# Issuing block 0's mask work earlier: one copy moved up on ScalarE, one product moved ahead of two weight loads on GpSimd

## The chip, the cores and the metric

The kernel runs on one core of one Trainium2 chip. The metric is the device time of one execution in microseconds (us). "The span" is the time from the first to the last recorded instruction of the profiled execution; it is some 2 us shorter than the device time. Every run also has a mean granted TensorE clock, where 1.0 is full speed.

The engines are called as the profile calls them: PE (TensorE matmul), PEld (its weight loads), DVE (VectorE), ACT (ScalarE), POOL (GpSimd), SP (SyncE).

## The reference

A linear attention with decay (4 batches, 8 heads, 768 positions, head size 64) is followed by a gated feed-forward layer on 3072 tokens (512 to 1536 to 512). Cut to what matters:

```python
intra = einsum(q_blk, k_blk) * Dmask        # decayed causal scores inside a block
intra = einsum(intra, v_blk)
inter = einsum(q_blk * lam_pow, kv_state)   # state from earlier blocks; zero for block 0
out   = intra + inter
...
gate = 1 / (1 + exp(-(x @ w_gate)));  val = x @ w_val
return (gate * val) @ w_out
```

## The kernel before

The kernel works in six blocks of 128 positions. The program gives each engine a list of instructions, and POOL's records up to 32 us start in the order of its list. In block 0 the attention has to be finished for all four batches before the first dense matmul (`gp`, the gate product; `vp` is the value product) can start. The stretch up to there is called the ramp below, and `ft` counts the slices of 128 of the 1536 columns; one load of WG or WV, called a weight slice, holds two of them. A load has landed when its data are in place. One batch goes through these steps:

- `piece_tq0`, `piece_tk0`: PE transposes q and k; DVE and ACT copy them out of PSUM as QS and KS.
- `piece_s`: PE computes the scores `sp`, in two halves (two heads that share a partition block).
- `piece_m` or `piece_m2`: the scores times the mask give `MT`. `piece_m` does both halves on DVE. `piece_m2` does half 0 on DVE; half 1 is copied from PSUM by ACT (`sc`) and multiplied by POOL.
- `piece_a`: PE multiplies by v (`op`), ACT copies the result into `XT`, which the dense matmuls read.

POOL also issues the loads of q, k, v and of the weights. That takes it 0.7 to 1.2 us each for most of them, and its products queue between these issues (the trace below has 0.76 to 0.81 us for a weight issue).

```python
    def piece_m2(n, b):
        MT[n, b] = mtp.tile([128, 2, HP, C], BF16, tag="MT", name="MT")
        nc.vector.tensor_tensor(out=MT[n, b][:, 0], in0=SP[n, b][0], in1=mask[:, 0], op=ALU.mult)
        sc = const.tile([128, HP, C], FP32, tag="sc", bufs=2)
        nc.scalar.copy(sc, SP[n, b][1])
        nc.gpsimd.tensor_tensor(out=MT[n, b][:, 1], in0=sc, in1=mask[:, 1], op=ALU.mult)
    # ...
    GW = DFF // 6
    load_gv(0, GW)            # weights WG, WV of ft 0 and 1: two DMA issues on POOL
    # ... transposes and scores of batch 0 (cut)
    piece_s(0, [1])
    piece_tk0(1)              # k of batches 2 and 3: two KS copies on ACT
    piece_tq0([2])
    piece_m2(0, 1)
    load_gv(1, GW)
    load_gv(2, GW)
    idle(3)                   # dummy matmuls on zeros
    piece_tq0([3])
    piece_s(0, [2], ps_ff, "ff")
    piece_m2(0, 2)
    piece_s(0, [3])
    piece_m(0, 3)
    idle(3)
    piece_a(0, [0])
    piece_a(0, [1])
    idle(2)
    piece_a(0, [2])
    piece_a0(3)
    idle(2)
    make_kd(0)                # POOL
    # ... further loads (cut), then the dense part
    gv(0, 0, 1, 2, 3)         # per ft: four gp matmuls, sigmoid, four vp matmuls, product
```

Of the kernel before, what the change touches and what calls it, by code (L numbers as in the profile page):

```python
# [11 lines left out]
ALU = mybir.AluOpType  # L12
# [4 lines left out]
def kernel(  # L17
# [11 lines left out]
    nc = tc.nc  # L29
# [52 lines left out]
    def load_gv(i, w):  # L82
        fs = slice(i * w, (i + 1) * w)
        nc.gpsimd.dma_start(out=WG[:, :, fs], in_=wg_r[:, :, fs])  # L84
        nc.gpsimd.dma_start(out=WV[:, :, fs], in_=wv_r[:, :, fs])  # L85
# [43 lines left out]
    for hp in range(HP):  # L129
# [6 lines left out]
    mask = const.tile([128, 2, HP, C], FP32, tag="mask")  # L136
    nc.vector.tensor_tensor(out=mask, in0=tri.unsqueeze(1).unsqueeze(1).to_broadcast([128, 2, HP, C]),
                            in1=pk.rearrange("p (g u) -> p u g", u=2).unsqueeze(3).to_broadcast([128, 2, HP, C]),
                            op=ALU.mult)
# [3 lines left out]
    def idle(n):  # L143
        for i in range(n):
            nc.tensor.matmul(wm, lhsT=zero[:, :128], rhs=zero, start=True, stop=True,  # L145
                             skip_group_check=True)

    QS, KS, MT, XT, KD = {}, {}, {}, {}, {}
# [12 lines left out]
    def piece_tq0(bs):  # L161
        tq = ps_at.tile([128, 2, HP, C], BF16, name="tq", tag="ps")
        for b in bs:
            if (0, b // 2) not in QS:
                QS[0, b // 2] = trsb.tile([128, 2, HP, C], BF16, tag="QS", name="QS")
            for hp in range(HP):
                nc.tensor.transpose(tq[:, b % 2, hp, :], Q[0][:, b, 2 * hp:2 * hp + 2, :], ident)
        for b in bs:
            nc.vector.tensor_tensor(out=QS[0, b // 2][:, b % 2], in0=tq[:, b % 2], in1=lamq, op=ALU.mult)

    def piece_tk0(bp):
        tk = ps_at.tile([128, 2, HP, C], BF16, name="tk", tag="ps")
        for i in range(2):
            for hp in range(HP):
                nc.tensor.transpose(tk[:, i, hp, :], K[0][:, 2 * bp + i, 2 * hp:2 * hp + 2, :], ident)
        KS[0, bp] = trsb.tile([128, 2, HP, C], BF16, tag="KS", name="KS")
        for i in range(2):
            nc.scalar.copy(KS[0, bp][:, i], tk[:, i])  # L178
# [21 lines left out]
    SP, OP = {}, {}  # L200

    def piece_s(n, bs, pool=ps_at, tag="ps"):

        for b in bs:
            bp, i = b // 2, b % 2
            sp = [pool.tile([128, HP, C], FP32, name=f"sp{u}", tag=tag) for u in range(2)]
            for hp in range(HP):
                for u in range(2):
                    us = slice(u * 64, (u + 1) * 64)
                    nc.tensor.matmul(sp[u][:, hp, :], lhsT=KS[n, bp][us, i, hp, :],  # L210
                                     rhs=QS[n, bp][us, i, hp, :],
                                     start=(hp == 0), stop=(hp == HP - 1), skip_group_check=True)
            SP[n, b] = sp

    def piece_m2(n, b):
        MT[n, b] = mtp.tile([128, 2, HP, C], BF16, tag="MT", name="MT")
        nc.vector.tensor_tensor(out=MT[n, b][:, 0], in0=SP[n, b][0], in1=mask[:, 0], op=ALU.mult)
        sc = const.tile([128, HP, C], FP32, tag="sc", bufs=2)
        nc.scalar.copy(sc, SP[n, b][1])
        nc.gpsimd.tensor_tensor(out=MT[n, b][:, 1], in0=sc, in1=mask[:, 1], op=ALU.mult)  # L220

    def piece_m(n, b):
        MT[n, b] = mtp.tile([128, 2, HP, C], BF16, tag="MT", name="MT")
        for u in range(2):
            nc.vector.tensor_tensor(out=MT[n, b][:, u], in0=SP[n, b][u], in1=mask[:, u], op=ALU.mult)  # L225
# [110 lines left out]
    GW = DFF // 6  # L336
# [7 lines left out]
    piece_s(0, [0])  # L344
    piece_m(0, 0)
    piece_s(0, [1])
    piece_tk0(1)
    piece_tq0([2])
    piece_m2(0, 1)
    load_gv(1, GW)  # L350
    load_gv(2, GW)
    idle(3)
    piece_tq0([3])
    piece_s(0, [2], ps_ff, "ff")
    piece_m2(0, 2)
    piece_s(0, [3])
    piece_m(0, 3)
    idle(3)
# [154 lines left out]
```

## Time and profile before

| | before |
|---|---|
| device time, median of 3 runs at the time of the prediction | 238.61 us (237.46 to 238.71) |
| span of the profiled run | 236.2 us |
| PE busy | 226.0 us, 96% |
| longest stop of PE after its start | 2.63 us, 15.86 to 18.50 |
| time at half clock inside the kernel | 3.41 us, 18.83 to 22.25 |

The first view is the timeline of the kernel before. Columns: start us, length us, engine, line, operation, output<-input, shapes, count; in brackets the engine's idle time before it and what ended that.

```profile
12.21 0.60 ACT L219 COPY sc<-sp 128x512 f32<-128x512 f32 x1
12.90 1.27 POOL L220 TENSOR_TENSOR MT<-sc,mask 128x512 bf16<-128x512 f32 x1 [0.95 <-ACT sc L219]
13.31 0.59 ACT L219 COPY sc<-sp 128x512 f32<-128x512 f32 x1 [0.50 <-PE sp L210]
14.11 0.81 POOL L84 DMA_DIRECT2D WG<-in_moe_w_gate_dram  x1
14.92 0.76 POOL L85 DMA_DIRECT2D WV<-in_moe_w_val_dram  x1
15.65 0.77 POOL L84 DMA_DIRECT2D WG<-in_moe_w_gate_dram  x1
16.38 0.78 POOL L85 DMA_DIRECT2D WV<-in_moe_w_val_dram  x1
17.14 1.31 POOL L220 TENSOR_TENSOR MT<-sc,mask 128x512 bf16<-128x512 f32 x1
18.50 0.38 PE L238 MATMUL op<-MT,vb 128*64 128x128 bf16 x7 [2.63 <-POOL MT L220]
20.00 1.91 PE L297 MATMUL gp<-XT,WG 128*128 128x512 bf16 x4
21.71 1.29 PE L303 MATMUL vp<-XT,WV 128*128 128x512 bf16 x4
22.84 1.03 PE L297 MATMUL gp<-XT,WG 128*128 128x512 bf16 x4
```

Two things are to be seen. The input of POOL's second product, the second `sc`, is ready at 13.90, but the product starts at 17.14, because four weight issues stand ahead of it in POOL's program: for 3.2 us its data are ready, and it overtakes none of the issues. And the first `gp` and `vp` groups are slow: four `gp` take 1.91 us by their records, where the next four take 1.03.

The second view is the table by stretches. The columns are the stretch, its length, busy us (and count) of PE, PEld, DVE, ACT and POOL, the granted clock, the DMA share (the packets' times over the time of 16 engines; a share above 1, such as the 2.14 of the first line, means that packets overlap), and GB/s.

```profile
11.93:15.34 3.41, 3.22 (x45) 1.62 (x42) 3.19 (x6) 1.84 (x4) 2.46 (x4) 1.00 2.14 168
15.34:18.75 3.41, 0.78 (x12) 0.36 (x12) 0.00 (x0) 0.71 (x2) 3.41 (x5) 1.00 1.45 196
18.75:22.17 3.42, 3.42 (x21) 1.29 (x16) 0.42 (x1) 1.08 (x3) 3.42 (x2) 0.51 1.42 192
```

The clock records of the trace start at 5.18, 18.83 and 22.25 us: 1.0 for 13.653 us, 0.5 for 3.413, then 1.0 for 215.040. These lengths are 4, 1 and 63 times 3.413, so the instants lie on one grid of 3.413 us; its steps are called grid windows below. (The stretches shown were cut 0.08 us early, hence the 0.51.) In the grid window from 15.42 PE worked only 0.78 us; in the next window the clock is half. The three windows before, from 5.18, 8.59 and 12.01, held 2.10, 2.60 and 3.22 us of PE work, and none was followed by a drop. So PE's stop seems to cost twice: 2.63 us of waiting, and then slow matmuls (1.91 us against 1.03 for four `gp`).

### The profile page before, as it was taken

To read this page: it belongs to the slowest core of one execution; us is meant where nothing else is said; L and a number is where in the kernel's file an instruction comes from. 1 tells how busy PE (TensorE), PEld (TensorE's weight loads), DVE (VectorE), ACT (ScalarE), POOL (GpSimd) and SP (SyncE) were. 2 spreads that over 40 slices of the span, in tenths; PEclk is the share of its full clock that TensorE was granted. 3 is DMA by queue.
4 is the path that set the end of the run, shared out by engine and by line. 5 is a ranking of instruction groups with operands and counts; after the bars stand their busy time and mean duration, and the time that the engine had idled before them with its cause. 6 is when DMAs were issued, how large, how long until landed. Compare 5 with 4: busy or idle time off the path is not lost.

```text
span 236.2 us, 3854 instructions
## 1 busy us (share of the span) xinstructions
PE 226.0 (96%) x1554; PEld 115.8 (49%) x1554; DVE 106.0 (45%) x185; ACT 80.8 (34%) x147; POOL 84.3 (36%) x73
## 2 busy tenths in 40 slices
PE   7768999999999999999999999999999999999993
PEld 2433445688644455544455544455544455444441
DVE  4351485574674250654750654750654750243300
ACT  5542334545331133433223333223333224433220
POOL 8989997770199000398000398000000000000000
PEclk9997999999999999999999999999999999999999
DMA  9999999999935993939982749992730012100022
GB/s 58 143 180 157 159 190 158 199 180 157 142 68 70 170 215 125 158 67 88 157 69 89 164 62 85 156 72 89 160 66 0 0 44 92 44 0 3 0 89 89
DMA packets 102321, 24.89 MB, mean 105 GB/s; under 512 B 91552, under 2 KB 99232, under 8 KB 102304
## 3 DMA queue, kind: packets, MB, share of 16 engines
q0 software_dynamic: 82064, 14.16, 80.8%
q1 hardware_dynamic: 20240, 10.49, 19.8%
q8 instruction: 12, 0.20, 0.4%
q14 instruction: 5, 0.04, 0.1%
HBM read 28.32 MB, written 6.29 MB: 147 GB/s over the span
## 4 chain that ended last, share of the span: by engine, by line
PE 91%; POOL 3%; DMA 3%; ACT 1%; issue 1%; POOLq 0%
PE po L329 27%; PE gp L297 24%; PE vp L303 24%; PE vp L320 3%; PE op L238 3%; DMA kb<-in_k_dram 3%; PE gp L314 2%; PE sp L210 2%; PE op L231 2%; PE cp L277 2%; POOL MT L220 1%; POOL WG L84 1%; POOL WV L85 1%; POOL kb L78 0%; ACT KS L178 0%
## 5 line engine op out<-in xcount | busy, mean ns | idle before, releaser
L306 DVE TENSOR_TENSOR ht<-sg,vp 128x512 bf16<-128x512 bf16 x65 | 44.7, 688 | 87.0 <-PE vp L303 86.7
L297 PE MATMUL gp<-XT,WG 128*128 128x512 bf16 x260 | 67.7, 383 | 0.0
L303 PE MATMUL vp<-XT,WV 128*128 128x512 bf16 x260 | 67.0, 380 | 0.0
L329 PE MATMUL po<-WO,ht 128*128 128x512 bf16 x288 | 65.2, 379 | 0.0
L300 ACT ACTIVATE sg<-gp 128x512 bf16<-128x512 f32 x65 | 38.8, 597 | 75.9 <-PE gp L297 75.8
L329 PEld LDWEIGHTS <-ht 128*128 128x128 bf16 x288 | 27.1, 98 | 32.2
L303 PEld LDWEIGHTS <-WV 128*128 128x128 bf16 x260 | 25.6, 99 | 31.1 <-issue 0.8
L297 PEld LDWEIGHTS <-WG 128*128 128x128 bf16 x260 | 24.8, 99 | 27.8 <-issue 1.1
L269 POOL TENSOR_TENSOR sd<-Sb,dec 128x512 f32<-128x512 bf16 x16 | 16.2, 1038 | 56.9 <-DVE Sb L286 56.9
L225 DVE TENSOR_TENSOR MT<-sp,mask 128x512 bf16<-128x512 f32 x44 | 27.8, 683 | 13.7 <-PE sp L210 13.7
L332 ACT COPY ob<-po 128x512 f32<-128x512 f32 x24 | 14.1, 586 | 54.5 <-PE po L329 50.7
L260 POOL TENSOR_TENSOR kd<-kb,kds 128x2048 bf16<-128x2048 bf16 x5 | 18.1, 3626 | 2.8 <-DMA kb<-in_k_dram 2.8
L245 ACT CAST XT<-op 128x512 bf16<-128x512 f32 x23 | 12.4, 588 | 7.4 <-PE op L238 7.4
L286 DVE TENSOR_TENSOR Sb<-cp,sd 64x256 bf16<-64x256 f32 x32 | 13.4, 420 | 0.8
L78 POOL DMA_DIRECT2D qb<-in_q_dram x9 | 12.5, 1387 | 0.8 <-POOLq L497 0.8
L78 POOL DMA_DIRECT2D vb<-in_v_dram x9 | 12.2, 1368 | 0.0
L78 POOL DMA_DIRECT2D kb<-in_k_dram x8 | 11.5, 1442 | 0.0
L145 PE MATMUL wm<-zero 128*128 128x512 bf16 x26 | 9.2, 489 | 1.2 <-DVE zero L97 1.2
L238 PE MATMUL op<-MT,vb 128*64 128x128 bf16 x184 | 7.6, 222 | 2.6 <-POOL MT L220 2.6
L324 DVE TENSOR_TENSOR ht<-sg,vp 128x256 bf16<-128x256 bf16 x14 | 5.8, 420 | 6.2 <-PE vp L320 3.8
L320 PE MATMUL vp<-XT,WV 128*128 128x256 bf16 x56 | 8.4, 272 | 0.1
L314 PE MATMUL gp<-XT,WG 128*128 128x256 bf16 x56 | 8.4, 273 | 0.0
(58 smaller groups left out, 114.4 us busy)
## 6 DMA issues: line engine op xcount, KB each, us to landing
out_dram<-ob SPq DMA_DIRECT2D x24, 256.0 KB, 2.0
qb<-in_q_dram POOLq DMA_DIRECT2D x4, 512.0 KB, 7.9
kb<-in_k_dram POOLq DMA_DIRECT2D x4, 512.0 KB, 10.0
vb<-in_v_dram POOLq DMA_DIRECT2D x4, 512.0 KB, 12.5
WG<-in_moe_w_gate_dram POOLq DMA_DIRECT2D x6, 256.0 KB, 6.6
WV<-in_moe_w_val_dram POOLq DMA_DIRECT2D x6, 256.0 KB, 7.2
WO<-in_moe_w_out_dram POOLq DMA_DIRECT2D x3, 512.0 KB, 14.8
kb<-in_k_dram POOLq DMA_DIRECT2D x4, 256.0 KB, 6.2
```

Of the source, the lines that this page charges most:

```text
L78: nc.gpsimd.dma_start(out=t[:, b0:b1], in_=src[b0:b1, :, sl, :].rearrange("b h s d -> s (b h) d"))
L225: nc.vector.tensor_tensor(out=MT[n, b][:, u], in0=SP[n, b][u], in1=mask[:, u], op=ALU.mult)
L238: nc.tensor.matmul(OP[n, b][us, hp, :], lhsT=V[n][:, b, 2 * hp + u, :], rhs=MT[n, b][:, u, hp, :], start=(n == 0 and hp == 0), stop=(hp == ...
L260: nc.gpsimd.tensor_tensor(out=KD[n], in0=K[n], in1=kds.unsqueeze(1).unsqueeze(3).to_broadcast([128, B, H, D]), op=ALU.mult)
L269: nc.gpsimd.tensor_tensor(out=SD[b], in0=Sb[:, b], in1=dec.unsqueeze(2).to_broadcast([128, HP, 128]), op=ALU.mult)
L297: nc.tensor.matmul(gp, lhsT=WG[:, mt, fs], rhs=x[:, mt, :], start=(mt == 0), stop=(mt == NMT - 1))
L300: nc.scalar.activation(sg, gp, AF.Sigmoid)
L303: nc.tensor.matmul(vp, lhsT=WV[:, mt, fs], rhs=x[:, mt, :], start=(mt == 0), stop=(mt == NMT - 1))
L306: nc.vector.tensor_mul(HT[n, ft], sg, vp)
L320: nc.tensor.matmul(vp[:, cs], lhsT=WV[:, mt, fs], rhs=x[:, mt, cs], start=(mt == 0), stop=(mt == NMT - 1))
L329: nc.tensor.matmul(po, lhsT=HT[n, ft][:, tt * 128:(tt + 1) * 128], rhs=WO[:, ft, :], start=(ft == 0), stop=(ft == NFT - 1))
L332: nc.scalar.copy(ob, po)
```

## The change

The intent: POOL's two mask products should not wait behind things they do not need. ACT copies `sc` of batch 1 before the second pair of KS copies, so that POOL can start its first product earlier. POOL does its second product ahead of the last pair of weight issues, and no longer behind it. Nothing is added or removed. A listing of each engine's instructions shows that PE and DVE keep their order.

```diff
-    def piece_m2(n, b):
+    def piece_m2(n, b, part):
+        if part:
+            nc.vector.tensor_tensor(out=MT[n, b][:, 0], in0=SP[n, b][0], in1=mask[:, 0], op=ALU.mult)
+            return
         MT[n, b] = mtp.tile([128, 2, HP, C], BF16, tag="MT", name="MT")
-        nc.vector.tensor_tensor(out=MT[n, b][:, 0], in0=SP[n, b][0], in1=mask[:, 0], op=ALU.mult)
         sc = const.tile([128, HP, C], FP32, tag="sc", bufs=2)
 ...
     piece_s(0, [1])
+    piece_m2(0, 1, 0)
     piece_tk0(1)
     piece_tq0([2])
-    piece_m2(0, 1)
+    piece_m2(0, 1, 1)
     load_gv(1, GW)
-    load_gv(2, GW)
     idle(3)
     piece_tq0([3])
     piece_s(0, [2], ps_ff, "ff")
-    piece_m2(0, 2)
+    piece_m2(0, 2, 0)
+    piece_m2(0, 2, 1)
+    load_gv(2, GW)
     piece_s(0, [3])
```

## The prediction

Its expectation that the clock stays up with a full window rests on the trace of before alone, in which windows with 2.10 to 3.22 us of PE work kept 1.0 and the one with 0.78 did not. Its "backlogged" rests on the third slices of WG and WV, which took 6.6 and 7.2 us from issue to landing in that trace, while 256 KB at the 193 GB/s of that stretch (15.65 to 22.20) would, by an estimate, take 1.4.

> **What bounds the kernel now.** TensorE: the page gives PE 226.0 of 236.2 us (96%). Only the ramp before the dense gate/value matmuls (first `gp`, 20.2 us) can give anything. In the timeline PE stands still once for long: 2.63 us, 15.86 to 18.50, where block 0's `op` for batch 2 waits for Pool's mask product `MT` (the waits view names it). The chain there reads: tk transposes, two KS copies on Scalar (11.25 to 12.32), `sc` copy (to 12.81), Pool `MT` of batch 1 (12.90 to 14.17), four weight issues on Pool (14.11 to 17.16), Pool `MT` of batch 2 (17.14 to 18.45), `op`. Pool idles 0.95 us before its first product, for `sc`.
>
> A second cost hangs on this gap: the granted clock is 0.50 from 18.75 to 22.17, so the first four `gp` take 1.71 us and the first four `vp` 1.09, later groups 0.86. [...] the low clock lasts 3.413 us, and the window before it (15.34 to 18.75) holds 0.75 us of PE work.
>
> **What the change moves.** Nothing is added or removed; PE and DVE keep their order.
> 1. Scalar: `sc` of batch 1 goes ahead of the second KS copies. Its `sp` ends about 10.45, Scalar is free, the copy takes 0.60: done about 11.1, before tk (11.25), so KS is not delayed. Pool's first product starts when the first weight issues end, about 11.92 instead of 12.90: −0.98.
> 2. Pool: the second product goes ahead of two weight issues (0.73+0.76): −1.49. It runs about 14.67 (`sc` ready at 13.90) to 15.98, not to 18.45.
>
> So `op` resumes at 16.03, 2.47 us earlier; V landed about 15.6, so no DMA takes over. With that window full the clock should stay up: `gp` starts about 17.4 (XT-bound), first `gp`+`vp` take 1.72 instead of 2.80. The second `gp` group starts about 19.1 instead of 23.0: **3.9 us**, 2.47 from the order, 1.4 from the clock.
>
> **Does it last?** Landings (issue plus time to landing): first weight slice WG/WV 16.9/18.2, needed 17.4/18.25, just fits. Second 19.6/20.9, needed 20.8/21.7; third 22.3/23.6 (issued 0.4 later, but the queue is backlogged), needed 24.7/25.5. Later ones are issued about 0.95 earlier; fourth 24.8/26.8, needed 28.6/29.5. Tightest: block 1's k for batches 2, 3, landing 42.9, then 41.9, needed about 42.1. New waits of 0 to 0.5 us may appear. After that PE is the limit and keeps the gain.
>
> **Prediction.** 238.61 − 3.9 = 234.7 us (1.6% faster); 8 in 10: 233.7 to 236.1. Over 2% faster 0.10, within 2% 0.89, slower 0.01.
>
> **What would show it.** The wait of `op` for `MT` falls from 2.6 to under 0.4; Pool's idle before `MT` gone; Pool products near 11.9 and 14.7; clock 1.0 between 18 and 23 us; first `gp` near 17.4, second near 19.1; later blocks' PE durations the same; span 236.2 to about 232.3.
>
> **What would make it wrong.** Weights landing late (PE waiting for WG or WV at 17 to 19 us) would give back up to 1 us. [...] runs of before differ by 1.25 us (237.46 against 238.7), which I take for runs without and with the low clock; without it only 2.5 us are to be had. If the clock still drops in the ramp, 1.4 us are lost. Late k at 42 us could swallow some of the gain.

## The result, and the profile after

The changed kernel takes 235.27 us (median of 4 runs, 234.83 to 235.56), the kernel before 238.66 (median of 4). The ratio is 0.9867, with a 95% interval of 0.9831 to 0.9904. Ratios here and below are the mean time of one kernel's fast runs over that of the other's fast runs of the same rounds, so they are not quite the ratio of the medians. The record calls a run slow when it lies over 1.5% above the fastest run of its kernel; none of the quoted runs does. A gain of 1.3% is clear of the noise.

Timeline of the changed kernel, the lines that answer to those above:

```profile
10.55 0.59 ACT L221 COPY sc<-sp 128x512 f32<-128x512 f32 x1 [0.49 <-PE sp L210]
11.91 1.34 POOL L222 TENSOR_TENSOR MT<-sc,mask 128x512 bf16<-128x512 f32 x1
13.13 0.84 POOL L84 DMA_DIRECT2D WG<-in_moe_w_gate_dram  x1
13.94 0.78 POOL L85 DMA_DIRECT2D WV<-in_moe_w_val_dram  x1
14.69 1.32 POOL L222 TENSOR_TENSOR MT<-sc,mask 128x512 bf16<-128x512 f32 x1
15.84 0.61 PE L240 MATMUL op<-MT,vb 128*64 128x128 bf16 x8
15.91 0.81 POOL L84 DMA_DIRECT2D WG<-in_moe_w_gate_dram  x1
17.17 1.02 PE L299 MATMUL gp<-XT,WG 128*128 128x512 bf16 x4
18.39 1.04 PE L305 MATMUL vp<-XT,WV 128*128 128x512 bf16 x4 [0.20 <-DMA WV<-in_moe_w_val_dram]
19.27 1.03 PE L299 MATMUL gp<-XT,WG 128*128 128x512 bf16 x4
```

POOL's products start at 11.91 and 14.69, `op` no longer stops, and the first `gp` group has the length of the later ones. There is a new wait: the first `vp` could start at about 18.03 (17.17 plus 0.86, the step of the later groups), but starts at 18.39, when its weights land. The profile books 0.20 us of this as PE idle.

The two grid windows of before, taken from the changed kernel (same columns; its own grid lies elsewhere, with steps at 14.10, 17.51 and 20.92):

```profile
15.34:18.75 3.41, 3.21 (x28) 1.27 (x27) 0.48 (x2) 2.31 (x5) 3.40 (x4) 1.00 1.45 199
18.75:22.17 3.42, 3.42 (x18) 1.57 (x16) 1.38 (x2) 0.79 (x3) 3.42 (x3) 1.00 1.40 187
```

The clock stays at 1.0. The chain of waits of the changed kernel from 10 to 24 us (an excerpt) shows what bounds the ramp now (start us, length us, what):

```profile
10.46 0.69 POOL WG L84
11.16 7.19 DMA WV<-in_moe_w_val_dram
18.35 0.05 issue
18.39 1.04 PE vp L305 x4
19.43 0.86 PE gp L299 x4
```

By these chains the second `gp` group started at 23.00 before and starts at 19.43 now: 3.57 us. The span fell by the same amount (236.2 to 232.6), so in this pair of profiles the later parts kept the gain of the ramp.

### The profile page after: what moved, and what is told of

It is laid out like the page before. It is cut to its first block, busy times and chain, and to the rows that moved or that the text cites. A ratio compares the mean times of both kernels' runs of the same rounds, so it can differ in the third digit from the quotient of the medians.

```text
span 232.6 us, 3855 instructions
## 1 busy us (share of the span) xinstructions
PE 224.0 (96%) x1554; PEld 115.1 (49%) x1554; DVE 106.0 (46%) x185; ACT 80.9 (35%) x147; POOL 84.4 (36%) x73
## 4 chain that ended last, share of the span: by engine, by line
PE 90%; POOL 4%; DMA 3%; issue 1%; ACT 0%; POOLq 0%
PE po L331 27%; PE vp L305 24%; PE gp L299 24%; DMA WV<-in_moe_w_val_dram 3%; PE vp L322 3%; PE gp L316 3%; PE op L240 2%; PE sp L210 2%; PE cp L279 2%; PE op L233 2%; POOL vb L78 1%; POOL qb L78 1%; POOL kb L78 1%; PE tk L196 0%; PE tq L190 0%
## 5 line engine op out<-in xcount | busy, mean ns | idle before, releaser
L299 PE MATMUL gp<-XT,WG 128*128 128x512 bf16 x260 | 66.8, 379 | 0.0
L145 PE MATMUL wm<-zero 128*128 128x512 bf16 x26 | 8.1, 441 | 1.2 <-DVE zero L97 1.2
```

Of the source, the lines that this page charges most:

```text
L299: nc.tensor.matmul(gp, lhsT=WG[:, mt, fs], rhs=x[:, mt, :], start=(mt == 0), stop=(mt == NMT - 1))
```

## The experiments

My theory was that of the prediction: about 2.5 us from the new order, 1.4 us from the clock that stays up, and a small loss to the first WV slice. The rival was that the low clock is a symptom without a price of its own. Kernels of one call ran on the same chip. All kernels gave the correct result except `no_wv_wait`.

### One half of the change at a time

`pool_only` has POOL's new order with ACT's old one; `scalar_only` has ACT's new order with POOL's old one.

```diff
 # pool_only, against the changed kernel
-    piece_m2(0, 1, 0)
     piece_tk0(1)
     piece_tq0([2])
+    piece_m2(0, 1, 0)
     piece_m2(0, 1, 1)
 # scalar_only, against the changed kernel
     load_gv(1, GW)
+    load_gv(2, GW)
 ...
     piece_m2(0, 2, 1)
-    load_gv(2, GW)
```

> Pool's new order alone, Scalar's order as before. My theory (order plus clock): Pool's first product stays at 12.90, the second runs 15.65 to 16.96, op of batch 2 resumes near 17.0, TensorE idles about 1.15 us instead of 2.63; the window 15.34 to 18.75 is then two thirds busy, the clock stays at 1.0, first gp near 18.3, second gp group near 20.1 against 22.84 before: 2.8 us faster than before, 0.8 slower than the changed kernel. Rival (the clock is worth nothing, only the order counts): 1.5 us faster than before.

> Scalar's new order alone, Pool's order as before. Pool's products at 11.9 and 16.17 to 17.48, op of batch 2 resumes near 17.5, idle about 1.65 us. Order alone is worth 1.0 us. If the clock stays at 1.0 (the window holds about half of its length in work; I can't say on which side that falls) the second gp group starts near 20.6 and the gain is 2.3 us; if it drops at 18.75 the gain is about 0.8 us. Rival (no worth of the clock): 1.0 us either way.

`pool_only`: 236.03 us, ratio 0.9879 (0.985 to 0.9907). `scalar_only`: 235.94 us, ratio 0.9873 (0.9841 to 0.9906). The kernel before had 238.71 on this chip, so each half alone is worth 2.7 to 2.8 us. PE's waits from 16 us on were, in `pool_only` and then in `scalar_only` (total us, times, longest):

```profile
PE op L240 <- POOL MT L222: 1.2, 1, 1.2
```

```profile
PE op L240 <- POOL MT L222: 0.8, 1, 0.8
```

In both profiles the clock stayed at 1.0 through the ramp (and no run of the eight had a mean clock below 0.998); the grid windows with the stop held 2.25 and 2.63 us of PE work. The rival had predicted 1.5 and 1.0 us, and it falls. My theory said 2.8 for `pool_only`, as measured, and at most 2.3 for `scalar_only`, which gained half a microsecond more; why is not known. The two halves do not add up (2.7 plus 2.8 against 3.4 for both in the first runs), since either one already shortens the stop (to 1.2 and 0.8 us) enough to keep the clock up, and that part can be won only once. In the profiled run of `scalar_only` the k of batches 2 and 3 also landed later (transposes at 11.57, not 10.60), so PE came to its stop later; that run's 0.8 us is smaller than the order alone would give, and it says nothing of the other three runs.

### The clock alone

`before_warm` is the kernel before with ten more dummy matmuls in PE's stop.

```diff
     piece_a(0, [1])
-    idle(2)
+    idle(12)
     piece_a(0, [2])
```

> The kernel before with ten more dummy matmuls on zeros (2.2 us) in the time that TensorE waits for Pool's second product. No order of Scalar or Pool changes: op of batch 2 still resumes at 18.50. My theory: the clock stays at 1.0, first gp near 19.85, second gp group near 21.5 instead of 22.84, 1.3 us faster than before. Rival (the low clock is only a symptom): no change, or slower by the dummy work.

> Before with ten more dummy matmuls, beside the changed kernel on one chip, to split the gain: clock part (before to this) 1.4, order part (this to the changed kernel) 2.5 if the prediction's term is right, about 2.0 if the landing of WV cut it by some 0.4.

Time: 237.19 us, ratio 0.9938 (0.9907 to 0.997), and on a second chip 236.92, ratio 0.9955 (0.9929 to 0.9981). The dummies did not always hold the clock: one of four runs and one of six had a mean clock of 0.990 or 0.989, and these two took 238.36 and 237.78 us. The timeline of `before_warm`:

```profile
15.54 2.76 PE L145 MATMUL wm<-zero 128*128 128x512 bf16 x12
18.97 0.38 PE L238 MATMUL op<-MT,vb 128*64 128x128 bf16 x7 [0.50 <-POOL MT L220]
20.07 1.02 PE L297 MATMUL gp<-XT,WG 128*128 128x512 bf16 x4
20.93 1.03 PE L303 MATMUL vp<-XT,WV 128*128 128x512 bf16 x4
21.80 1.03 PE L297 MATMUL gp<-XT,WG 128*128 128x512 bf16 x4
```

`op` resumes even a little later than before (18.97 against 18.50), yet the second `gp` group starts at 21.80 instead of 22.84. Useless work made the kernel faster, so the low clock has a price of its own.

The runs of the kernel before that went with the experiments say the same without any edit. That the loss lies in the ramp is taken from the one profile. Of 34 runs on three chips, 28 had a mean clock of 0.993 or less and a mean time of 238.7 us; 6 had a mean clock of 1.0 and a mean time of 237.2. The shares differed between chips: 0 of 11, 4 of 11, 2 of 12. The instant at which the grid falls differed between traces too (modulo 3.413 us it is 1.77 in the trace before and 0.44 in the trace after). One drop (3.41 us at half clock, of a span of 236.2) takes 0.007 off a run's mean clock; no run of the changed kernel, of 15, was below 0.996 (the clock also falls at the very end of a run: in its first profile at 232.55 of 232.63 us), so none had a drop in the ramp.

### The changed kernel on other chips

> The changed kernel unaltered, as the measure for the other runs of this call. Expected 235.2, clock 1.0 in the ramp. My theory of its spread (234.8 to 235.6): the first WV slice lands at other times in other runs, and the first vp waits for it.

> The changed kernel unaltered, the measure of this call: about 235.1, clock 1.0, a wait of vp for WV of 0.2 to 0.5 us.

Times: 234.97 us, ratio 0.9872 (0.9846 to 0.9899), and 234.64, ratio 0.9842 (0.9809 to 0.9875). The gain of some 3.1 to 3.9 us in the medians repeats. The first `vp` waits again in both, as seen in PE's waits from 16 us on, first of `after_same_chip`, then of `after_third`:

```profile
PE vp L305 <- DMA WV<-in_moe_w_val_dram: 0.4, 1, 0.4
```

```profile
PE vp L305 <- DMA WV<-in_moe_w_val_dram: 0.3, 1, 0.3
```

The call of `after_same_chip` also held `before_warm_again`, which splits the gain on one chip. Runs of before with the low clock averaged 238.38 (7 runs), `before_warm_again` without a drop 236.88 (5 of its 6 runs), the changed kernel 235.05 (5 runs). By this measure the clock is worth 1.5 us, against 1.4 predicted, and the order 1.8, against 2.5 predicted. The record allows a second measure, in which no dummies take part: the kernel before in its own runs at full clock. On this chip these average 237.30 us (4 runs, 236.87 to 238.04), which makes the clock 1.1 us and the order 2.2; on the chip of `after_third` (2 runs, 237.03) it makes them 1.8 and 2.3. Both parts are shown to exist, but the split is known to about half a microsecond only.

### Asking for the first WV slice later

`gate_pair` runs the two gate products of ft 0 and 1 before their two value products, so WV is needed 0.86 us later.

```diff
-    gv(0, 0, 1, 2, 3)
+    gv01(0)          # gp of ft 0, gp of ft 1, then vp of ft 0, vp of ft 1
+    gv(0, 2, 3)
```

> The changed kernel with the two gate products of the first slice ahead of its two value products, so that WV of the first slice (lands near 18.4) is needed at 18.9 instead of 18.0. My theory (0.36 us of the predicted 3.9 were lost to that landing, and nothing later takes it back): vp of ft 0 starts without a DMA wait, third gp group near 20.6 instead of 20.99, 0.3 to 0.4 us faster than the changed kernel. Rival (a later landing, block 1's k near 42 us or the second slice, or Pool, takes it back): no change against the changed kernel.

> The kernel of gate_pair again, since its profile fell on a run with a low clock from 12.6 to 16.0 us. My theory: a profile without that drop shows no wait for WV, and the time is 0.3 to 0.4 below the changed kernel of this call. Rival (the wait is only moved): equal within 0.15.

`gate_pair`: 234.86 us, ratio 0.9841 (0.9815 to 0.9867), in a call without the changed kernel. `gate_pair_again`, beside the changed kernel: 234.84 against 234.97. The means are 234.84 and 235.05; one run of the six had a low clock (0.993) and took 235.53. In that profile the first `vp` group did not wait, but the `vp` of the next slice did:

```profile
PE op L240 <- POOL MT L222: 0.2, 1, 0.2
PE vp L305 <- DMA WV<-in_moe_w_val_dram: 0.2, 1, 0.2
```

So a part of the wait moved on. The profile of the first `gate_pair` fell on a run with half clock from 12.58 to 15.99 us (236.18 us): three dummies from 12.58 took 1.47 us, where three from 11.99 took 0.81 in the changed kernel. The grid window before that held 1.90 us of PE work, part of it transposes (columns: stretch, length, PE busy and count, clock, DMA share, GB/s):

```profile
9.17:12.58 3.41, 1.90 (x31) 1.00 2.35 150
```

`gate_pair_fill` adds two dummy matmuls there, where PE waits for the second k.

```diff
     piece_m2(0, 1, 0)
+    idle(2)
     piece_tk0(1)
```

> gate_pair with two more dummy matmuls where TensorE waits for the second k, to keep the clock up in runs like the profiled one of gate_pair. Expected: median equal to gate_pair_again within 0.15, no run above 235.5; rival: the dummies delay the second tk and cost 0.2.

It took 234.78 us (234.55 to 235.0), and no run showed a drop (lowest mean clock 0.997). That is 0.2 us below the changed kernel of the same call, less than the spread of the runs. By means it is 234.77 here, 234.70 in `gate_pair_again` without its low-clock run, and 235.05 in the changed kernel (5 runs each): on this chip 0.3 us may have been won, as the theory had it.

### Taking the wait for WV away altogether

In `no_wv_wait` the value products of ft 0 to 3 of block 0 read the gate weights, so nothing waits for the first two WV slices. Its output is wrong, which doesn't matter for the time.

```diff
-   nc.tensor.matmul(vp, lhsT=WV[:, mt, fs], rhs=x[:, mt, :], ...)
+   nc.tensor.matmul(vp, lhsT=(WG if n == 0 and ft < 4 else WV)[:, mt, fs], rhs=x[:, mt, :], ...)
```

> The changed kernel, but the value products of ft 0 to 3 of block 0 read the gate weights, so that nothing waits for the first two WV slices; the result is wrong on purpose. My theory: the landing of WV is what kept the gain below the predicted 3.9; 0.4 us (0.3 to 0.6) faster than the changed kernel of this call. Rival (a bound other than WV takes its place, or the wait overlaps another): under 0.15.

It took 234.71 us against 234.64 of the changed kernel beside it (means 234.72 and 234.69): no gain, and this theory of mine falls. Its timeline shows the expected early start, and where the gain went (PEld lines are weight loads; at 20.86 and 39.55 the wait, 0.58 and 0.26 us, is booked on them):

```profile
18.02 1.03 PE L305 MATMUL vp<-XT,WG 128*128 128x512 bf16 x4
18.88 1.03 PE L299 MATMUL gp<-XT,WG 128*128 128x512 bf16 x4
20.86 0.55 PEld L299 LDWEIGHTS <-WG 128*128 128x128 bf16 x4 [0.58 <-DMA WG<-in_moe_w_gate_dram]
39.55 0.47 PEld L240 LDWEIGHTS <-vb 128*64 128x64 bf16 x16 [0.26 <-DMA vb<-in_v_dram]
42.88 0.62 PE L196 MATMUL tk<-ident,kb 128*128 128x128 bf16 x8 [0.41 <-DMA kb<-in_k_dram]
```

The second `gp` group is 0.39 us ahead of the first profile of the changed kernel (18.88 against 19.27). At the third, which waits for the second WG slice, 0.13 us are left (20.86 against 20.99), and at the `op` of block 1, which waits for v, nothing (39.55 against 39.52). PE then comes to block 1's k of batches 2 and 3 before that has landed, and starts on it 0.61 us later than in that profile. So three later landings, not one, stand behind the first; `after_third`, of the same call, reaches these places later (19.49, 21.21, 39.74), and against it only the k takes the lead away. In the profiles that leave the later program as it was, the span is the start of these transposes plus 190.3 to 190.4 us (six are shown; the others of this kind fit too):

| profile | start of block 1's second k transposes in the timeline, us | span, us |
|---|---|---|
| before | 45.85 | 236.2 |
| pool_only | 43.46 | 233.8 |
| changed kernel | 42.27 | 232.6 |
| after_same_chip | 42.89 | 233.2 |
| after_third | 42.61 | 232.9 |
| no_wv_wait | 42.88 | 233.2 |

In the first profile of the changed kernel there is no room at this place. Its timeline shows POOL's `kd`, which waits for the same k, and PE's transposes starting together:

```profile
42.23 3.62 POOL L262 TENSOR_TENSOR kd<-kb,kds 128x2048 bf16<-128x2048 bf16 x1 [3.17 <-DMA kb<-in_k_dram]
42.27 0.61 PE L196 MATMUL tk<-ident,kb 128*128 128x128 bf16 x8
```

Before, the two were at 42.91 and 45.85. The order of the ramp can move the start of the transposes only down to the landing. `after_third`, of the chip of `no_wv_wait`, has no room either (42.63 and 42.61). But `after_same_chip` has:

```profile
42.06 3.62 POOL L262 TENSOR_TENSOR kd<-kb,kds 128x2048 bf16<-128x2048 bf16 x1 [2.57 <-DMA kb<-in_k_dram]
42.89 0.61 PE L196 MATMUL tk<-ident,kb 128*128 128x128 bf16 x8
```

There the k had landed 0.83 us before PE came, so the k was no bound; it is the chip on which the two `gate_pair` versions came out 0.3 us lower by their means. Whether that bound takes the gain thus seems to depend on the run; this was not tested.

### Both at once

`gate_pairs` pairs ft 2 and 3 as well. `late_k` takes `gate_pair_fill` and moves block 1's second transposes behind one half-size gate/value group, with one more ft split in halves.

```diff
 # gate_pairs, against gate_pair_fill (gv_pair is gv01 for any two ft)
-    gv01(0)
-    gv(0, 2, 3)
+    gv_pair(0, 0)
+    gv_pair(0, 2)
 # late_k, against gate_pair_fill
-    t(1, 1)
     load(2, "qkv", 0, B)
     transpose_by_dma(2)
-    gvh(1, 0, 0, 1)
+    gvh(1, 0, 0)
+    t(1, 1)
+    gvh(1, 0, 1, 2)
     sc(1, 1)
 ...  (m and a one group later too; ft 7 split in halves)
```

> gate_pair_fill with the slices of ft 2 and 3 paired too, so that the second WV slice is needed later as well (the profile of gate_pair_again has its vp waiting for it). Correct result. My theory: no wait for either WV slice, 0.3 to 0.5 faster than the changed kernel of this call, near no_wv_wait. Rival: no better than gate_pair_fill, about 0.25 faster.

> gate_pair_fill with block 1's second transposes (which need the k of batches 2 and 3, landing at 42.1 to 42.9 in the traces) moved behind one half gate/value group, about 0.9 us, and one more ft split in halves so that the rest keeps its cover. Correct result. In every profile so far the span is the start of those k transposes plus 190.3 us. My new theory: two DMA landings in a row bound the start, WV of the first slice and this k, so taking away the first alone gave nothing in no_wv_wait; with both away no wait for k is left, and the time is 0.3 to 0.6 under the changed kernel's 234.97 (mean of 15 runs), so 234.4 to 234.7. Rival (the start is set elsewhere, on TensorE or at Pool): 234.8 as gate_pair_fill, or above it because of the extra half-size matmuls.

`gate_pairs` took 235.12 us (234.5 to 236.23), not better than the 234.64 of the changed kernel beside it. Its profile shows no DMA wait of PE from 16 us on (span 232.7); its slow runs were not profiled, and their clock was 1.0. `late_k` took 234.85 us, on the chip on which the changed kernel had 234.64: no gain either. Its profile fell on the slowest of its six runs (235.67), and PE had one wait from 16 us on:

```profile
PE vp L324 <- DMA WV<-in_moe_w_val_dram: 0.8, 1, 0.8
```

There is no wait for k, as meant. But in this run the first WV slice took 8.9 us from issue to landing, where it took 7.2 in the changed kernel's first profile. It came at 20.04 us, and the 0.86 us that the pairing gives were not enough. The landing times of the ramp differ between executions by more than the 0.4 us at issue, and no version beat the changed kernel beyond doubt.

## Why the prediction was right

- **The stop of `op` behind POOL's products.** Right. The prediction had the products at 11.92 and 14.67, and they are at 11.91 and 14.69. `op` was to resume at 16.03; its group starts at 15.84 (15.62 before) and runs through without a stop past the end of POOL's product at 16.01. KS was not delayed by the copy put ahead of it: ACT had finished that copy at 11.14 and was idle for 0.32 us when the second k transposes were done.
- **The clock.** Right that the low clock costs time of its own: 1.4 us predicted, 1.5 measured with dummy matmuls in place of the change, and 1.1 and 1.8 on two chips from the runs of before at low and at full clock. That is 0.5% to 0.7% of 238 us, but a third or more of this change's gain. The remark that runs of before without the low clock exist was right as well (6 of 34, 237.2 us). For the 237.46 of the first rounds it stays a guess, as that run's clock was not recorded.
- **The sum.** 3.9 us predicted; 3.57 between the two first profiles, 3.4 between the medians. Its "first weight slice WG/WV 16.9/18.2, needed 17.4/18.25, just fits" did not fit: WV landed about 18.35 and was needed about 18.03, since `gp` started at 17.17 and not at 17.4. In this pair of profiles that wait of 0.36 us is the whole difference: the first `gp` starts 2.83 us earlier (20.00 to 17.17), the first `gp` and `vp` take 0.74 less (2.84 to 2.10), and 0.36 more would make 3.93. The order's 2.47 us measured 1.8 us against the kernel with dummies, 2.2 and 2.3 against before at full clock. The wait is about half of what is lacking by the first measure, and all of it by the second.
- **The later landings.** The prediction named block 1's k as the tightest, landing at 41.9 and needed at 42.1. It landed near 42.2 and was needed at that moment. The profile of `no_wv_wait` shows it as a bound behind the first, along with the second WG slice and v: what is won at WV is given back at these. In `after_same_chip` the k was no bound.
- **What stays open.** Whether removing the bounds together pays was not settled, since landings vary by up to 1.7 us between the profiled runs (18.4 to 20.0 for the first WV slice, which took 7.2, 7.8, 7.4 and 8.9 us from issue to landing in the three profiles of the changed kernel and in `late_k`). Why they vary was not tested. How much PE work in a grid window keeps the clock up is not shown either: windows with 0.78 us (before) and 1.90 (`gate_pair`) were followed by a drop, windows with 1.89 (`scalar_only`, from 7.74), 2.25 (`pool_only`) and 2.63 (`scalar_only`) were not; those of 1.90 and 1.89 hold transposes too. Nor is it known why some runs of `gate_pairs` were slow at full clock.

## What to carry to other kernels

On POOL, which here both computes and issues loads, the order counted: one product stood 3.2 us behind four issues with its data ready. Where an engine does both, put a product whose consumer is stopped ahead of issues whose data is needed later, and read off the timeline when its inputs were ready. A stop of PE can cost twice (here 2.63 us of waiting, and 1.1 to 1.8 us of slow matmuls after it), so look at the granted clock just after it, and test with dummy matmuls what the clock alone is worth. When a wait goes away, check each later landing for its slack: here, in the first profile, PE waited for the first WV slice and reached block 1's k within 0.04 us of its landing, and on the chip where this was tested taking the first wait away gained nothing.
